# Retention and an ELU feed-forward block on one core: outputs leave PSUM later, M4's input differences come earlier, ELU buffers from two pools, M7's small weights in the second block's first GEMM

## The chip, the core and the metric

The kernel runs on one core of one Trainium2 chip. The metric is device time in microseconds, a median over runs. One execution of the kernel before was profiled; all durations and views below are from that one. In the views PE is TensorE's matmuls, PEld its weight loads, DVE is VectorE, ACT is ScalarE, POOL is GpSimd and SP is SyncE, whose queue (SPq) issues all the DMAs here.

## The reference

```python
# retention: B=4, H=8, S=768, D=64
gamma = 1.0 - 2.0 ** (-5.0 - np.arange(H))
for t in range(S):
    state = gamma * state + k[t] (outer) v[t]
    y[t]  = q[t] @ state / sqrt(D)
# bridge: x = y as (3072 tokens, 512)
h = x @ w_in                       # 512 -> 2048
g = np.where(h > 0.0, h, np.exp(np.minimum(h, 0.0)) - 1.0)
out = g @ w_out                    # 2048 -> 512
```

All of it is in FP32.

## The kernel before

**Blocks.** The 3072 tokens are worked in six blocks of 512 (`tb` 0 to 5). For every block the kernel does the retention of 4 chunks of 128 tokens (scores, states, outputs), then the first GEMM with the ELU, then the second GEMM and the stores. Retention of block `tb + 1` is woven into the GEMMs of block `tb`. The order on every engine is written out by hand: generators (`yield`) are advanced step by step, each engine takes its instructions in program order, and waits follow from the tiles read and written.

**Strassen products.** GEMMs are done with seven products P1 to P7 instead of eight. Block 0 has plain products in its first GEMM and one Strassen level in the second. Block 1 has one level in its first GEMM (four column groups `n` = 0 to 3, functions `first` and `strassen`) and two levels in its second. Blocks 2 to 5 have a first GEMM that is partly two levels deep (`unit`) and a second GEMM of two levels: `second_twice` runs the seven outer products M1 to M7 in the order `ORDER2` = 1, 2, 3, 7, 6, 5, 4 (places `at` = 0 to 6), each an `inner` of seven products with four 128x128x128 FP32 matmuls.

**Inner products and banks.** An `inner` is P1 (bank "a"), P2 ("b"), P6 ("a"), P7 ("d"), P5 ("a"), P3 ("a"), P4 ("d", added to P7). Its P3 and P4, the tail, run after P1 and P2 of the next `inner`. DVE reads bank "d" twice: `res[1,1]` (L1011, shown at L881, the helper `add`) after P5, `res[1,0]` after P4. The loop calls `work(at)` for early and late DVE work: `inputs_of(j)` makes the four input differences `ts` of a coming outer product (L853), `form(j)` differences of whole GEMM results (L790), `next_x` the differences `xt` of the next block's input (L467). `visit(at, where)` puts retention steps in: `outputs` has DVE multiply the PSUM result `y` into `xb` (L397, four operations). `bring` loads the chunks of the block after next (1 MB each) and has POOL scale their v (L285).

**Weights.** The sums of weights that the inner products need ("small weights") are made by DVE, sent to DRAM (`to_send`, `send_small`) and fetched back, 256 KB each, through a ring of 11 tiles `wq` (`fetch_small`, L822 and L827): a fetch is issued when a tile has been used. For the first GEMM of the later blocks `combine_small(j)` makes four sums for j = 2, 3, 7, 4 (L839) and stores 1 MB. M2's and M3's are made in block 1's first GEMM, in tiles `wi` of the pool `stage`; M7's and M4's in block 1's second GEMM, in the memory of `xt`. After the first GEMM the pool is closed and the ring takes its memory:

```python
    early.close()
    ring = ctx.enter_context(tc.tile_pool(name="ring", bufs=RING))
    tpool = ctx.enter_context(tc.tile_pool(name="tpool", bufs=2))
    for _ in range(RING):
        fetch_small()
```

**ELU.** `elu` has ACT make max(-h, 0) and its exponential in a buffer `r`; DVE then joins it with h (L494). `r` comes from `epool`, with three buffers. In `strassen` with `behind` false (n = 1 to 3) the result C11 is P1, copied by ACT to SBUF, plus P2 by DVE (`plus`, L708).

Of the kernel before, what the change touches and what calls it, by code (L numbers as in the profile page):

```python
# [9 lines left out]
FP32 = mybir.dt.float32  # L10
# [8 lines left out]
def kernel(  # L19
# [357 lines left out]
    def outputs(tb, pp):  # L377

        y = [ps_r.tile([P, 2 * 2, 2, D], FP32, name="y", tag="r") for _ in range(2)]
        for x in range(2):  # L380
            for j in range(4):
                pt = raw[tb * CPB + 2 * pp + j // 2][0][:, 1].rearrange("p h c -> p (h c)")
                within(tb, pp, x, j, y, lambda p: pt[:, (x * HP + p) * D :][:, 0:D])
        for other in range(2):
            if not other:
                yield
            else:

                for sub in range(2):
                    seen = epool.tile([P, 8], FP32, name="seen", tag="seen")  # L390
                    nc.vector.tensor_copy(seen.rearrange("p (j x) -> p j x", x=2), y[sub][:, :, :, 0])
                yield
            for x in range(2):
                across(tb, pp, x, other, y)
        i = chunks[tb * CPB + 2 * pp][1]
        for sub in range(2):
            nc.vector.tensor_tensor(  # L397
                out=place_of(x_of(tb)[:, :, 2 * pp * C : 2 * (pp + 1) * C])[:, :, :, sub, :], in0=y[sub],
                in1=place_of(powers[:, :, i * C : (i + 2) * C])[:, :, :, sub, :], op=ALU.mult,
            )  # L400
# [11 lines left out]
    def across(tb, pp, x, other, y):  # L412
        q = raw[tb * CPB + 2 * pp + x][0]
        for u in range(2):
            for a in range(2):
                sub = a ^ other
                n = 4 * pp + 2 * x + sub
                if fresh(tb, n):
                    continue
                for c in range(2):  # L420
                    p = 2 * u + c
                    nc.tensor.matmul(
                        y[sub][rows(c), 2 * a + u, x, :], lhsT=state(tb, n)[rows(a), p, :],
                        rhs=q[rows(a), 0, p, rows(sub)], start=False, stop=True, skip_group_check=True,
                    )
# [56 lines left out]
        while later:  # L482
            later.pop(0)()

    def elu(g, h, depth=1, then=None):


        r = epool.tile([P, 512], FP32, name="r", tag="r", bufs=3)
        e = r if len(h.shape) == 2 else r.rearrange("p (a c) -> p a c", c=P)
        nc.scalar.activation(e, h, AF.Relu, scale=-1.0)  # L490
        nc.scalar.activation(e, e, AF.Exp, scale=-1.0)  # L491

        def last():
            nc.vector.scalar_tensor_tensor(g, e, -1.0, h, ALU.add, ALU.max)  # L494
            if then:
                then()

        while len(later) >= depth:
            later.pop(0)()
        later.append(last)  # L500
# [210 lines left out]
    def strassen(product, use, behind):  # L711


        yield
        pa = bank("a")
        product(1, pa, True)
        m1 = kept(pa)
        yield
        pb = bank("b")
        product(2, pb, True)  # L720
        h = plus(pb, m1)
        if not behind:
            use("C11", h)
        yield
        product(6, pa, False)
        u2 = kept(pa)
        if behind:
            use("C11", h)
        yield
        pd = bank("d")  # L730
        product(7, pd, True)
        yield
        product(5, pa, False)
        u4 = kept(pa)
        use("C22", plus(pd, u4))
        yield "gap"
        product(3, pa, False)
        use("C12", pa)
        yield
        product(4, pd, False)  # L740
        h = plus(pd, u2)
        yield "last"
        use("C21", h)
# [200 lines left out]

    def elu_of(j, r, t):
        g = place(UNITS[j][0][0], r, t)
        elu(g, g, 4)

    def first_one(n, j, ps):

# [232 lines left out]
    def run(steps):  # L1183
        for _ in steps:
            pass
# [12 lines left out]
    for n, _ in enumerate(inner):  # L1198
        if n in (0, 2, 4):
            load(CPB + n // 2)  # L1200
        if n == 4:
            load(CPB + 3)
        if n in (1, 2, 4, 5, 7, 9):
            next_piece(n in (1, 2, 5, 7))
        if n in (3, 5, 7, 9):
            scale_v(CPB + (n - 3) // 2)
        if n == 4:
            run(inputs_of_first(0, [hslot() for _ in range(3)]))
        elif n == 10:
            scores(1, 0)  # L1210
            scores(1, 1)
        elif n == 11:
            states(1, 0)
            states(1, 1)
            next_piece()
            parts = sums_of_pieces(0)
            next(parts)
        elif n == 12:
            outputs_step(1, 0)
            run(parts)  # L1220
            next_piece()
        elif n == 13:
            outputs_step(1, 1)
            smalls = small_of_pieces(0)
            some(smalls, 3)
        elif n == 14:
            outputs_step(1, 2)
            some(smalls, 2)
            decode_all()
        elif n == 15:  # L1230
            run(smalls)
# [43 lines left out]
    def retention_step(tb, step):  # L1275
        if tb >= NTB:
            return
        if step == 0:
            scores(tb, 0)
            scores(tb, 1)  # L1280
        elif step == 1:
            states(tb, 0)
            states(tb, 1)
        elif step < 5:
            outputs_step(tb, step - 2)


    tail = iter(())
    last = held["last"]
    sides = [  # L1290
        itertools.chain(combine_w_in(1), last), itertools.chain(combine_w_in(2), combine_w_in(3)), iter(()), iter(()),
    ]
    smalls = {2: combine_small(2), 3: combine_small(3)}
    some(smalls[2], 1)
    for n in range(NQ):
        if n < 3:
            load(2 * CPB + n)
        if n == 2:
            load(2 * CPB + 3)
        cur = first(n)  # L1300
        for at in range(3):
            next(cur)

        if n in (1, 2):
            some(smalls[n + 1], 1)
        elif n == 3:
            scale_v(2 * CPB, True)
        for _ in tail:
            pass
        for at, s in enumerate(cur):  # L1310
            next(sides[n], None)
            next(sides[n], None)
            if at == 1 and n in (0, 2):
                some(smalls[2 if n == 0 else 3], 2)
            elif at == 1 and n == 3:
                for m in range(1, CPB):
                    scale_v(2 * CPB + m, True)
            if s == "gap":
                break
        for _ in sides[n]:  # L1320
            pass
        tail = cur
        if n in (1, 2):
            run(smalls[n + 1])
        send_small()
# [14 lines left out]
            some(xt_parts[0], 2)  # L1340
        return [begin]

    smalls = {j: combine_small(j, xt_.rearrange("p j a (b c) -> p (j a b) c", c=P).rearrange("p (k f) c -> p k f c", k=4)) for j in (7, 4)}

    def small_part(j):
        def last():
            run(smalls[j])
            send_small()
        return 3 * [lambda: some(smalls[j], 1)] + [last]

    def work_of_second(at):
        i = lambda j: inputs_of(j, ts)
        return [
            ([], i(2)), (i(3), []), (i(7), small_part(7)), (form(6), i(6)), (i(5), small_part(4)), (form(4), i(4)),
            (next_x(), []),
        ][at]

    LOADS = {(4, "end"): (0, 1), (5, "middle"): (2, 3)}
# [1 line left out]
    def visit_of_second(at, where):  # L1360
        if (at, where) == (0, "tail"):
            next(tail)
            next(tail)
        elif (at, where) == (0, "middle"):
            for _ in tail:
                pass
            flush()
        if where == "end" and at < 5:
            retention_step(2, at)
        bring(3, at, where)  # L1370

    def bring(tb, at, where):
# [9 lines left out]
    for tb in range(2, NTB):  # L1382
# [72 lines left out]
        def work_of_second(at):  # L1455
            i = lambda j: inputs_of(j, ts)
            return [
                ([lambda: pop(2)], last_elus + i(2)), ([lambda: pop(2)] + i(3), form(5)), (form(7), i(7)), (form(6), i(6)),
                (i(5), form(4)), ([], i(4)), (next_x() if more else [], []),
            ][at]  # L1460

        def visit_of_second(at, where):
            if (at, where) == (0, "tail"):
                elu_of(3, 0, 0)
                elu_of(3, 1, 1)
                for _ in tail:
                    pass
            elif where == "end" and at in (1, 3, 4) and more:
                retention_step(tb + 1, {1: 2, 3: 3, 4: 4}[at])
            bring(tb + 2, at, where)  # L1470

        tail = second_twice(tb, ts, work_of_second, visit_of_second)
# [51 lines left out]
```

## Time and profile before

| | |
|---|---|
| Median of 3 runs | 644.95 us (644.07 to 645.58) |
| The profiled execution's own time | 639.73 us |
| Its span, first to last instruction | 638.0 us |
| Mean granted clock of TensorE | 1.000 |
| Busy: PE, DVE, ACT | 624.6, 510.0, 264.1 us |
| DMA moved | 146.83 MB, mean 230 GB/s |

A line of the timeline has the start, the duration, the engine, the line of the kernel, the operation, the tile written and the tiles read, shapes, the count of merged instructions, and in brackets the idle time before it with what ended it. A line of waits has the total, the times and the longest. A DMA line has the size and the median time from issue to landing.

### The profile page before, as it was taken

Reading aid. Unit: us, or ns where it says so; the run is one execution under the profiler, and the core shown is the slowest. Engines: PE = TensorE matmul, PEld = TensorE weight load, DVE = VectorE, ACT = ScalarE, POOL = GpSimd, SP = SyncE. Lnnn points to the kernel's source line nnn. Section 1 sums busy time; section 2 is a strip of 40 time slices with the busy share of each in tenths; the row PEclk is TensorE's granted clock in tenths of the full one; section 3 lists DMA queues with packets and bytes.
Section 4 is the critical chain, followed back from the end, with each engine's and each line's share of the span. In section 5 each row is a group of like instructions: output and inputs, shape, how many; then the busy total and the mean of one; then the engine's idle time right before and its main releaser. Section 6 shows DMA issues by size and latency. Waiting matters only on the chain.

```text
span 638.0 us, 16700 instructions
## 1 busy us (share of the span) xinstructions
PE 624.6 (98%) x6870; PEld 564.5 (88%) x6870; DVE 510.0 (80%) x930; ACT 264.1 (41%) x496; POOL 23.6 (4%) x30
## 2 busy tenths in 40 slices
PE   8999999999999989999899999999999999999997
PEld 6864578888899978999898999999899999899997
DVE  5678799989798787499869389988569887469995
ACT  5898645025631112565111367211257311357411
POOL 1021000000000011000002000002000000000000
PEclk9999999999999999999999999999999999999999
DMA  8698669689287997248789136789425888325894
GB/s 320 258 415 295 187 207 269 193 272 327 88 271 234 303 372 275 66 134 257 255 272 395 53 108 194 249 289 398 145 74 169 251 269 263 117 74 166 270 312 138
DMA packets 80794, 146.83 MB, mean 230 GB/s; under 512 B 6864, under 2 KB 32336, under 8 KB 75472
## 3 DMA queue, kind: packets, MB, share of 16 engines
q1 hardware_dynamic: 80720, 145.78, 68.7%
q8 instruction: 54, 0.88, 0.5%
q14 instruction: 20, 0.16, 0.1%
HBM read 122.42 MB, written 23.33 MB: 228 GB/s over the span
## 4 chain that ended last, share of the span: by engine, by line
PE 85%; DVE 9%; issue 2%; ACT 2%; DMA 1%; DVEq 0%
PE pa L984 17%; PE pd L984 9%; PE qa L956 7%; PE pa L896 5%; PE pa L757 4%; PE pb L984 4%; PE pa L956 3%; PE pa L534 3%; PE pb L956 3%; PE x L624 3%; PE pd L896 3%; DVE gC L881 2%; PE pd L757 2%; PE pa L624 2%; PE sc L311 2%; PE y L407 2%
## 5 line engine op out<-in xcount | busy, mean ns | idle before, releaser
L992 ACT COPY ms<-pa 128x128 f32<-128x128 f32 x104 | 27.4, 264 | 146.1 <-PE pa L984 135.5
L984 PE MATMUL pa<-ts,wq 128*128 128x128 f32 x560 | 74.1, 275 | 2.4 <-DMA wq<-scratch_dram 2.4
L984 PE MATMUL pd<-ts,wq 128*128 128x128 f32 x552 | 73.7, 277 | 1.6 <-DVE res L881 1.2
L984 PEld LDWEIGHTS pa<-ts,wq 128*128 128x128 f32 x560 | 68.2, 192 | 2.7 <-issue 2.6
L984 PEld LDWEIGHTS pd<-ts,wq 128*128 128x128 f32 x552 | 67.1, 192 | 3.0 <-DVE res L881 2.9
L984 PE MATMUL pa<-gC,wq 128*128 128x128 f32 x480 | 64.7, 277 | 0.8 <-DVE res L881 0.6
L491 ACT ACTIVATE r<-r 128x512 f32<-128x512 f32 x96 | 60.5, 630 | 3.1
L984 PEld LDWEIGHTS pa<-gC,wq 128*128 128x128 f32 x480 | 58.8, 192 | 2.0 <-DVE res L881 0.8
L490 ACT ACTIVATE r<-gC 128x512 f32<-128x512 f32 x64 | 40.1, 626 | 16.0 <-DVE gC L494 9.4
L881 DVE TENSOR_TENSOR res<-pd,ms 128x128 f32<-128x128 f32 x68 | 19.5, 287 | 32.0 <-ACT ms L992 17.7
L853 DVE TENSOR_TENSOR ts<-gC,ts 128x512 f32<-128x512 f32 x60 | 43.8, 730 | 1.0
L853 DVE TENSOR_TENSOR ts<-gC 128x512 f32<-128x512 f32 x60 | 42.0, 701 | 0.1
L494 DVE SCALAR_TENSOR_TENSOR gC<-r,gC 128x512 f32<-128x512 f32 x64 | 41.1, 682 | 0.6 <-ACT r L491 0.6
L881 DVE TENSOR_TENSOR gC<-pb,gC 128x512 f32<-128x512 f32 x20 | 13.3, 682 | 30.3 <-PE pb L896 30.3
L285 POOL TENSOR_TENSOR chunk<-chunk,vf 128x512 f32<-128x512 f32 x16 | 20.9, 1309 | 410.7 <-DVE ts L853 180.0
L896 PE MATMUL pa<-ts,wq 128*128 128x128 f32 x256 | 34.8, 279 | 0.0
L984 PE MATMUL pb<-gC,wq 128*128 128x128 f32 x240 | 31.9, 276 | 0.0
L896 PEld LDWEIGHTS pa<-ts,wq 128*128 128x128 f32 x256 | 31.1, 191 | 0.5
L984 PEld LDWEIGHTS pb<-gC,wq 128*128 128x128 f32 x240 | 29.4, 192 | 0.0
L1014 ACT COPY res<-pa 128x128 f32<-128x128 f32 x34 | 9.0, 266 | 40.9 <-PE pa L984 40.6
L881 DVE TENSOR_TENSOR res<-res 128x512 f32<-128x512 f32 (+1 forms) x31 | 22.0, 713 | 2.3 <-ACT ms L992 0.5
L790 DVE TENSOR_TENSOR gC<-gC,gC 128x512 f32<-128x512 f32 x36 | 22.4, 683 | 0.0
(274 smaller groups left out, 1259.5 us busy)
## 6 DMA issues: line engine op xcount, KB each, us to landing
wq<-scratch_dram SPq DMA_DIRECT2D x309, 256.0 KB, 4.4
chunk<-in_qkv_dram SPq DMA_DIRECT2D x22, 1024.0 KB, 8.9
wraw<-in_w_dram SPq DMA_DIRECT2D x15, 1024.0 KB, 6.0
out_dram<-res SPq DMA_DIRECT2D x14, 256.0 KB, 4.6
scratch_dram<-gT SPq DMA_DIRECT2D x12, 256.0 KB, 4.4
scratch_dram<-m SPq DMA_DIRECT2D x12, 192.0 KB, 6.3
scratch_dram<-so SPq DMA_DIRECT2D x4, 512.0 KB, 4.7
scratch_dram<-wi SPq DMA_DIRECT2D x2, 1024.0 KB, 6.7
```

The costliest lines, as they stand in the source:

```text
L490: nc.scalar.activation(e, h, AF.Relu, scale=-1.0)
L491: nc.scalar.activation(e, e, AF.Exp, scale=-1.0)
L494: nc.vector.scalar_tensor_tensor(g, e, -1.0, h, ALU.add, ALU.max)
L624: nc.tensor.matmul(X[j][:, d, :], lhsT=w[j][:, d * P : d * P + P], rhs=x[j], start=(n == 0 and d == 0), stop=at_end, skip_group_check=True,)
L757: nc.tensor.matmul(ps[:, fi, :], lhsT=w[:, fi, j2, :], rhs=x[:, j2, :], start=(begin and fi == 0 and j2 == 0), stop=(j2 == 1), skip_group_ ...
L790: nc.vector.tensor_tensor(out=gq[o][:, q], in0=gq[x][:, q], in1=gq[y][:, q], op=ALU.subtract)
L853: sub = lambda o, x, y: nc.vector.tensor_tensor(out=o, in0=x, in1=y, op=ALU.subtract)
L881: nc.vector.tensor_tensor(out=o, in0=x, in1=y, op=ALU.add)
L896: nc.tensor.matmul(ps[:, f, :], lhsT=lhs[f], rhs=xs[j][k], start=(begin and f == 0), stop=True, skip_group_check=True,)
L956: nc.tensor.matmul(ps[:, fi, :], lhsT=w[:, fi, j2, :], rhs=x[:, j2, :], start=(j == 1 and fi == 0 and j2 == 0), stop=(j2 == 1), skip_group ...
L984: nc.tensor.matmul(ps, lhsT=w[:, f, :], rhs=ts[j][k][:, f, :], start=(begin and f == 0), stop=(f == 3), skip_group_check=True,)
L992: nc.scalar.copy(m, ps)
```

## The change

1. `outputs` has one more step, for blocks 1 and later: the four multiplications out of PSUM (L397) are a step of their own. In the second GEMM they come at `(5, "first")`, behind the sum of the M6 result, instead of at the end of `at` = 4.
2. `inputs_of(4)` becomes early work of `at` = 5 instead of late work; in block 1 `form(4)` comes at the end of `at` = 4.
3. `elu_of` takes `r` from `hpool` for the quarters with r != t, and from `epool` for the others.
4. In `strassen` with `behind` false P1 is copied by ACT into bank "b" and P2 is added there by PE; the ELU of C11 reads the bank. P2 comes behind the tail of the group before.
5. `combine_small(7)` is run in block 1's first GEMM, n = 3, in a tile of `stage`, and sent there. In the second GEMM only `combine_small(4)` is left, at the place where M7's was.

```diff
@@ outputs
             for x in range(2):
                 across(tb, pp, x, other, y)
+        if tb:
+            yield
         i = chunks[tb * CPB + 2 * pp][1]
@@ elu
-    def elu(g, h, depth=1, then=None):
-        r = epool.tile([P, 512], FP32, name="r", tag="r", bufs=3)
+    def elu(g, h, depth=1, then=None, pool=None):
+        r = pool.tile([P, 512], FP32, name="r", tag="h") if pool else epool.tile([P, 512], FP32, name="r", tag="r", bufs=3)
@@ strassen
-        m1 = kept(pa)
-        yield
-        pb = bank("b")
-        product(2, pb, True)
-        h = plus(pb, m1)
-        if not behind:
-            use("C11", h)
+        if behind:
+            m1 = kept(pa)
+            pb = bank("b")
+        else:
+            pb = bank("b")
+            nc.scalar.copy(pb, pa)
+        yield
+        product(2, pb, behind)
+        if behind:
+            h = plus(pb, m1)
+        else:
+            use("C11", pb)
@@ elu_of
-        elu(g, g, 4)
+        elu(g, g, 4, pool=None if r == t else hpool)
@@ block 0's loop, n == 14
             outputs_step(1, 2)
+            outputs_step(1, 3)
@@ retention_step
-        elif step < 5:
+        elif step < 6:
             outputs_step(tb, step - 2)
@@ block 1, first GEMM
-        itertools.chain(combine_w_in(1), last), itertools.chain(combine_w_in(2), combine_w_in(3)), iter(()), iter(()),
+        itertools.chain(combine_w_in(1), last), itertools.chain(combine_w_in(2), combine_w_in(3)), iter(()), combine_small(7),
...
-        for at in range(3):
+        for at in range(2 if n else 3):
             next(cur)
...
         for _ in tail:
             pass
+        if n:
+            next(cur)
         for at, s in enumerate(cur):
...
             elif at == 1 and n == 3:
+                run(sides[3])
+                send_small()
                 for m in range(1, CPB):
                     scale_v(2 * CPB + m, True)
@@ block 1, second GEMM
-            ([], i(2)), (i(3), []), (i(7), small_part(7)), (form(6), i(6)), (i(5), small_part(4)), (form(4), i(4)),
-            (next_x(), []),
+            ([], i(2)), (i(3), []), (i(7), small_part()), (form(6), i(6)), (i(5), form(4)), (i(4), []), (next_x(), []),
...
         if where == "end" and at < 5:
             retention_step(2, at)
+        elif (at, where) == (5, "first"):
+            retention_step(2, 5)
@@ blocks 2 to 5, second GEMM
-                (i(5), form(4)), ([], i(4)), (next_x() if more else [], []),
+                (i(5), form(4)), (i(4), []), (next_x() if more else [], []),
...
             elif where == "end" and at in (1, 3, 4) and more:
                 retention_step(tb + 1, {1: 2, 3: 3, 4: 4}[at])
+            elif (at, where) == (5, "first"):
+                retention_step(tb + 1, 5)
```

More of the change, by code (lines that the diff above doesn't have):

```diff
@@ L1290 @@
     sides = [
-        itertools.chain(combine_w_in(1), last), itertools.chain(combine_w_in(2), combine_w_in(3)), iter(()), iter(()),
+        itertools.chain(combine_w_in(1), last), itertools.chain(combine_w_in(2), combine_w_in(3)), iter(()), combine_small(7),
     ]
-    smalls = {2: combine_small(2), 3: combine_small(3)}
+    smalls = {j: combine_small(j) for j in (2, 3)}
     some(smalls[2], 1)
@@ L1341, in next_x, with small_part @@
         return [begin]
-    smalls = {j: combine_small(j, xt_.rearrange("p j a (b c) -> p (j a b) c", c=P).rearrange("p (k f) c -> p k f c", k=4)) for j in (7, 4)}
-    def small_part(j):
+    last_small = combine_small(
+        4, xt_.rearrange("p j a (b c) -> p (j a b) c", c=P).rearrange("p (k f) c -> p k f c", k=4)
+    )
+    def small_part():
         def last():
-            run(smalls[j])
+            run(last_small)
             send_small()
-        return 3 * [lambda: some(smalls[j], 1)] + [last]
+        return 3 * [lambda: next(last_small)] + [last]
     def work_of_second(at):
```

## The prediction

> **What bounds the kernel.** I read the page first, then the waits of PE and of the DMA queue (SP), then the timeline round each place that the diff touches.
>
> ```profile
> PE 624.6 (98%) x6870; PEld 564.5 (88%) x6870; DVE 510.0 (80%) x930; ACT 264.1 (41%) x496; POOL 23.6 (4%) x30
> PE 85%; DVE 9%; issue 2%; ACT 2%; DMA 1%; DVEq 0%
> ```
>
> The busy line and the chain by engine: TensorE sets the time, and the number of its matmuls does not change. So only its waits can be won or added.
>
> ```profile
> PE pa L984 <- DMA wq<-scratch_dram: 2.4, 1, 2.4
> PE pd L984 <- DVE res L881: 1.2, 3, 0.5
> SPq L827 <- DMA scratch_dram<-wi: 4.9, 1, 4.9
> ```
>
> Waits (total, times, longest). PE waits once for a weight tile (2.4 us, at 231 in block 1) and a little for bank "d" to be read. The third line is the warning: the first ring fetch stood behind the landing of a stored `wi` tile.
>
> **1. M7's weights in the first GEMM (n = 3): +7.5 us.** In the built order of the changed kernel SP issues M7's store right ahead of the ring's first fetch, and that fetch waits on the store's landing, because the ring lies in the memory of the closed pool `stage`. M3's store has that place now:
>
> ```profile
> 167.95 0.68 DVE L839 TENSOR_TENSOR wi<-w_s,wi 128x512 f32<-128x512 f32 x1
> 168.66 0.33 SPq L656 DMA_DIRECT2D scratch_dram<-wi  x1
> 174.04 0.80 SPq L827 DMA_DIRECT2D wq<-scratch_dram  x2
> 178.01 1.05 PE L984 MATMUL pa<-gC,wq 128*128 128x128 f32 x8
> ```
>
> ```profile
> scratch_dram<-wi SPq DMA_DIRECT2D x1, 1024.0 KB, 5.3
> wq<-scratch_dram SPq DMA_DIRECT2D x2, 256.0 KB, 2.7
> scratch_dram<-xt SPq DMA_DIRECT2D x1, 1024.0 KB, 4.8
> ```
>
> The timeline, and issue to landing of these DMAs: store 168.7, landed 174.0, fetch, landed 176.6, first use at 177.8 (the weight load ahead of the 178.01 row). Slack 1.2 us.
>
> When does M7's store leave? Its four sums stand on DVE behind the ELU of n = 2's C21. PE runs P1(3), then n = 2's last two products, which end at 171.3 (each 1.73; today P2(3) is between and they end at 173.0). DVE then does the C21 sum at 171.3, C12's ELU 171.9, the two L769 sums 172.6 and 173.35, C21's ELU 174.0, and M7's four at 0.61 a start from 174.6: done 177.2. Store 5.3, fetch 2.7, start of PE 0.1: 185.3 instead of 177.8. PE has nothing else: the product stands ahead in its order. +7.5; low end 6.9 (the 4.8 row), high end 9.3 (a fetch at the page's median of 4.4). The ring's later tiles come 0.7 apart and are wanted 0.9 apart, so nothing more is lost.
>
> The wait's length raises the clock question. After the idle start of the program four 128-column matmuls take 1.11 us, where eight take 1.06 later; that slow pace runs from 1.45 to about 5.8 us and loses half of 4.4, 2.2 us. After the 2.4 us wait at 231 eight take 1.13, full pace.
>
> ```profile
> 5.14 1.11 PE L339 MATMUL pa<-so,chunk 128*128 128x128 f32 x4
> ```
>
> A wait of 7.5 us lies between these rows, so 0 to 2.2; I take the middle, +1.1. The Trainium skill ("TensorE: Matmul & The Clock Gate", Part 1: The HAM clock gate) says more: an idle window of about 3.4 us halves the clock, and about 3.4 us of work restores it. By that the loss would be an estimated 1.7 to 3.4 us, and the whole sum 0.6 to 2.3 higher.
>
> **2. M4's small sums where M7's were (block 1).** The 1 MB store ahead of the chunk loads at 222.7 goes, and with it the fetch wait at 231. The store moves on SP to 207.3, ahead of the fetches that M7's precedes today without a wait of PE, and the 2.5 us of sums move on DVE from 220 to 204.6; `form(4)` (2.5 us) comes up to their old place. What is won here is reckoned in 3, because a new wait comes first.
>
> **3. Outputs out of PSUM later, M4's input differences earlier (second GEMM, at = 4 to 6).** Block 2 today:
>
> ```profile
> 325.77 1.16 PE L984 MATMUL pa<-gT,wq 128*128 128x128 f32 x8
> 327.71 2.47 DVE L397 TENSOR_TENSOR xb<-y,etab 128x512 f32<-128x512 f32 x4
> 330.30 0.28 DVE L881 TENSOR_TENSOR res<-pd,ms 128x128 f32<-128x128 f32 x1
> 330.63 0.97 PEld L984 LDWEIGHTS pd<-ts,wq 128*128 128x128 f32 x8 [0.32 <-DVE res L881]
> 333.02 0.29 DVE L881 TENSOR_TENSOR res<-pd,ms 128x128 f32<-128x128 f32 x1 [1.65 <-ACT ms L992]
> 333.23 1.10 DVE L853 TENSOR_TENSOR ts<-gC 128x512 f32<-128x512 f32 x1
> 335.19 1.37 POOL L285 TENSOR_TENSOR chunk<-chunk,vf 128x512 f32<-128x512 f32 x1 [1.40 <-DVE ts L853]
> 335.58 1.53 DVE L853 TENSOR_TENSOR ts<-gC,ts 128x512 f32<-128x512 f32 x1
> 337.56 0.97 PEld L984 LDWEIGHTS pd<-ts,wq 128*128 128x128 f32 x8 [0.60 <-DVE res L881]
> ```
>
> At at = 5 the order is P1 (325.77), P2, at 4's P3 and P4, P6, P7, P5, then at 6's P1, P2, and at 5's P3, P4. P7 (its weight load is the row at 330.63) waits for the read of bank "d" at 330.30, which stands behind the four L397 (0.3 us); a second P7 waits at 337.56 because the `ts` sums were stretched beside POOL. Both waits go, as meant. But the changed DVE order at at = 5 is: sums of at 4, four L397, four `ts`, and only then `res[1,1]`, the second read of bank "d" after P5. At 5's P4 adds into that bank and waits for it.
>
> Without POOL, from P1's start: P4 of at 4 ends at +3.85, its read +3.9, `res<-res` +4.3, L397 +4.9 to +7.3, `ts` +7.3 to +9.9, the read +9.8 to +10.05, P4 +10.1, second P7 two products and one refill later, +12.0. Block 4 has no chunk loads; its second P7 starts at +11.2 (539.04 against 527.83): +0.8.
>
> With POOL (blocks 1 to 3) the `ts` sums are pinned: the first ends after POOL's first product, the last after its second, as today at 337.11. The read follows at 337.05 to 337.3, P4 at 337.4 instead of 335.2, second P7 at +13.5 against +11.8: +1.7. Block 3: `ts` end 438.25, P4 +11.8, second P7 +13.7 against 438.70 − 426.68 = 12.0: +1.7. Block 1: P7 at 234.65 − 220.57 = +14.1 today (0.4 for the bank, 2.6 for the fetch); I take +13.6: −0.5. Sum −0.5 + 1.7 + 1.7 + 0.8 = +3.7. Low end: `ts` never stretched, +12.0 everywhere: −2.1 + 0.2 + 0 + 0.8 = −1.1. High end: one more stretched operation (0.4) in three blocks, +4.9.
>
> **4. ELU buffers from two pools (blocks 2 to 5): −1.6 us.**
>
> ```profile
> 282.03 0.63 ACT L490 ACTIVATE r<-gC 128x512 f32<-128x512 f32 x1 [1.39 <-DVE gC L494]
> 283.23 0.58 ACT L910 COPY pb<-pa 128x512 f32<-128x512 f32 x1
> 283.87 1.16 PE L896 MATMUL pb<-xb,w_s 128*128 128x128 f32 x8
> ```
>
> ACT waits 1.39 us for the third ELU buffer; behind it stands the copy into "pb", and PE starts 0.33 late for it (0.23 wait, 0.10 refill), then 0.2 for the next ACT copy. At most 0.53 a block, four blocks: −2.1. DVE is the next late one at 281 to 283, so I take 0.4 each: −1.6; end 0.
>
> **5. P2 after the tail, C11 summed in PSUM: 0.** ACT copies "pa" to "pb" instead of to SBUF; the copy (0.58) is hidden by two products of 3.45 us, and three DVE sums of 0.61 go. The extra step of block 1's `outputs` in the first block runs right behind the step before it, so its order stays. C11 of n = 3 is ready only at 180.1 instead of 172.4, and the second inner product reads it: 1.3 us if the ring wait of part 1 did not cover it.
>
> **Sum.** 7.5 + 1.1 + 3.7 − 1.6 = +10.7 us on the profiled execution's 639.73 (span 638.0): 650.4. The median of the runs shown, 644.95, is 5.2 above that execution; the added waits are the same there: 655.6.
>
> **Rivals.**
> *No new wait for bank "d"*: if bank reads came in time, the second P7 would start at +10.8 (twelve products of 0.89 and a refill); blocks 1 to 4 would save 3.3, 1.0, 1.2 and 0.4, and the sum would be 7.5 + 1.1 − 5.9 − 1.6 = +1.1: 646.1. For it: no P4 waits today. Against it: the built order puts eight operations of 0.61 us, 4.9 us, between P4's old and new reads.
> *The store does not hold the ring* (faster): M7's store would have landed by 177.8. For it: DVE idles for 1.9 and 1.0 us at 166 to 170. Against it: the sums stand behind C21's ELU, in order. With zero wait C11 still costs 1.3; with the terms of 3 and 4 at their low ends the sum is 1.3 − 1.1 − 2.1 = −1.9: 643.0. With a ring wait w above 1.3 the sum is w − 3.2, so this decides for faster by over 0.2% once w is below 1.9 us.
> *The clock halves for the whole 4.4 us*: +1.1 more, 656.7, inside the range.
> *The edits do not do what they say*: the new ELU buffers share `hpool` with `m7` and the results; if a buffer were held by an output DMA, part 4 would be 0 or above: 657.2 or more. The output stores of block 2 are issued by 349 and the next unit's tiles come 15 us later, so it is unlikely.
>
> **How the numbers follow.** My forecast 0.80 (with either clock), no bank wait 0.10, no ring hold 0.05, the ELU rival 0.05. The forecast's ends are 644.95 + 6.9 + 0 − 1.1 − 2.1 = 648.7 and 644.95 + 9.3 + 2.2 + 4.9 = 661.4; 650.0 to 661.0 leaves out the two low rivals and little else. A difference under 0.2% (1.3 us) can't be told from none here. Slower 0.91: forecast, ELU rival and part of the first rival; same 0.04; faster 0.05.
>
> **What would show it.** Right: the first L984 product near 185 with a wait of 7 us for `wq`, after a `wi` store at 177; no fetch wait in block 1's end; P4 of at 5 waiting 1 to 2.5 us for `res` in blocks 1 to 4 and P7 not waiting; the ACT wait of 1.39 gone. Wrong: a first fetch before 178, or P4 starting on time.

## The result

The changed kernel takes 653.4 us (median of 4 runs, 652.47 to 656.6) beside 645.2 for the kernel before: a ratio of 1.0139 (95% interval 1.010 to 1.0178), 8 to 9 us slower. A second comparison gave 1.0134 (1.009 to 1.0178). The forecast was 655.6 in a range of 650.0 to 661.0. The profiled execution took 652.47 us with a span of 650.7. Line numbers have moved: the adds of L881 are now L888, the products of L984 L991, the differences of L853 L860, the outputs of L397 L399, the small sums of L839 L846, the fetches L829 and L834. A ratio is taken over all runs and is not the quotient of the two medians.

The page of the changed kernel, its busy line and its chain by engine:

```profile
PE 626.1 (96%) x6870; PEld 567.2 (87%) x6870; DVE 506.6 (78%) x927; ACT 263.9 (41%) x496; POOL 22.2 (3%) x30
PE 91%; DVE 4%; DMA 2%; issue 2%; DVEq 0%; SPq 0%
```

The count of TensorE's instructions is the same and its busy time is 1.5 us longer, while the span grew by 12.7. So most of the time, 11.2 us, was added in waits. DVE has three sums less, as the change says, and is 3.4 us less busy; TensorE's waits did not fall with it. The waits of the changed kernel (total, times, longest):

```profile
PEld pd L991 <- DVE res L888: 7.4, 5, 2.4
PE pd L991 <- DVE res L888: 6.5, 4, 2.2
PE pa L991 <- DMA wq<-scratch_dram: 6.1, 1, 6.1
```

Before, PE had 2.4 us for `wq` and 1.2 for bank "d". Now it waits 6.1 us for the first tile of the ring and four times for bank "d", up to 2.2 us. These are the two waits that were forecast.

**The ring.** The timeline of the changed kernel round the first product of block 1's second GEMM:

```profile
177.49 0.68 DVE L846 TENSOR_TENSOR wi<-w_s,wi 128x512 f32<-128x512 f32 x1
178.20 0.33 SPq L658 DMA_DIRECT2D scratch_dram<-wi  x1
182.26 0.80 SPq L834 DMA_DIRECT2D wq<-scratch_dram  x2
185.27 0.98 PE L991 MATMUL pa<-gC,wq 128*128 128x128 f32 x3 [6.10 <-DMA wq<-scratch_dram]
```

M7's last sum ends at 178.2, the store leaves with it and lands at 182.07, the fetch leaves at 182.26 and lands at 184.93, and the product starts 0.3 us later. The chain sums, store, fetch, product is as the prediction drew it; only the store is shorter (3.9 us for 5.3).

**The clock.** Windows behind the two longest waits (PE, PEld, DVE, ACT and POOL busy with counts, granted clock, DMA share, GB/s):

```profile
185.20:187.00 1.80, 1.73 (x8) 1.76 (x9) 0.00 (x0) 0.00 (x0) 0.00 (x0) 0.50 0.81 156
187.00:189.00 2.00, 2.00 (x12) 1.98 (x12) 0.00 (x0) 0.27 (x1) 0.00 (x0) 0.57 0.91 289
189.00:191.00 2.00, 2.00 (x11) 1.77 (x10) 0.89 (x2) 0.30 (x1) 0.00 (x0) 1.00 1.03 397
345.00:347.00 2.00, 2.00 (x12) 2.00 (x13) 0.65 (x3) 0.00 (x0) 0.00 (x0) 0.68 1.10 449
347.00:349.00 2.00, 2.00 (x11) 2.00 (x11) 1.07 (x2) 0.27 (x1) 0.00 (x0) 0.50 0.98 406
```

The granted clock is 0.5 for 3.4 us behind the wait of 6.1 us, as feared, and again behind the wait of only 2.2 us in block 2, which the prediction had not priced.

**Bank "d".** The same place in block 2 (P1 of `at` = 5 starts at 333.60):

```profile
338.48 2.48 DVE L399 TENSOR_TENSOR xb<-y,etab 128x512 f32<-128x512 f32 x4
340.38 1.04 POOL L285 TENSOR_TENSOR chunk<-chunk,vf 128x512 f32<-128x512 f32 x1 [89.86 <-DMA chunk<-in_qkv_dram]
340.87 1.09 DVE L860 TENSOR_TENSOR ts<-gC 128x512 f32<-128x512 f32 x1
342.83 1.36 POOL L285 TENSOR_TENSOR chunk<-chunk,vf 128x512 f32<-128x512 f32 x1 [1.41 <-PE pa L991]
343.21 1.53 DVE L860 TENSOR_TENSOR ts<-gC,ts 128x512 f32<-128x512 f32 x1
344.66 0.28 DVE L888 TENSOR_TENSOR res<-pd,ms 128x128 f32<-128x128 f32 x1
345.00 1.45 PE L991 MATMUL pd<-ts,wq 128*128 128x128 f32 x8 [2.20 <-DVE res L888]
```

`res[1,1]`, the read of bank "d" at 344.66, was ready to run at 340.4 (ACT's copy of P5 had ended). It stands behind four outputs and four differences, two of them stretched while POOL works, and P4 at 345.00 waits for it.

### The profile page after: what moved, and what is told of

Its sections match the earlier page's. It is cut to its first block, busy times and chain, and to the rows that moved or that the text cites. A ratio compares the mean times of both kernels' runs of the same rounds, so it can differ in the third digit from the quotient of the medians.

```text
span 650.7 us, 16691 instructions
## 1 busy us (share of the span) xinstructions
PE 626.1 (96%) x6870; PEld 567.2 (87%) x6870; DVE 506.6 (78%) x927; ACT 263.9 (41%) x496; POOL 22.2 (3%) x30
## 4 chain that ended last, share of the span: by engine, by line
PE 91%; DVE 4%; DMA 2%; issue 2%; DVEq 0%; SPq 0%
PE pa L991 18%; PE pd L991 9%; PE pa L903 9%; PE qa L963 6%; PE pd L903 4%; PE pb L991 4%; PE pa L764 4%; PE pa L963 3%; PE pa L536 3%; PE pb L963 3%; PE x L626 3%; PE pb L903 2%; PE pa L626 2%; PE kv L351 2%; PE y L409 2%; PE sc L311 2%
## 5 line engine op out<-in xcount | busy, mean ns | idle before, releaser
L991 PE MATMUL pd<-ts,wq 128*128 128x128 f32 x552 | 74.4, 278 | 6.5 <-DVE res L888 6.5
L991 PE MATMUL pa<-ts,wq 128*128 128x128 f32 x560 | 74.8, 277 | 0.0
L991 PEld LDWEIGHTS pd<-ts,wq 128*128 128x128 f32 x552 | 68.0, 194 | 7.5 <-DVE res L888 7.4
L991 PE MATMUL pa<-gC,wq 128*128 128x128 f32 x480 | 65.8, 280 | 7.2 <-DMA wq<-scratch_dram 6.1
L991 PEld LDWEIGHTS pa<-ts,wq 128*128 128x128 f32 x560 | 69.1, 194 | 0.1
L991 PEld LDWEIGHTS pa<-gC,wq 128*128 128x128 f32 x480 | 59.5, 194 | 8.8 <-issue 7.1
L888 DVE TENSOR_TENSOR res<-pd,ms 128x128 f32<-128x128 f32 x68 | 19.5, 287 | 37.7 <-PE pd L991 25.5
L860 DVE TENSOR_TENSOR ts<-gC,ts 128x512 f32<-128x512 f32 x60 | 43.5, 726 | 1.0
L860 DVE TENSOR_TENSOR ts<-gC 128x512 f32<-128x512 f32 x60 | 41.4, 690 | 1.2 <-DMA scratch_dram<-wi 1.0
L888 DVE TENSOR_TENSOR gC<-pb,gC 128x512 f32<-128x512 f32 x20 | 13.3, 681 | 30.3 <-PE pb L903 30.3
L285 POOL TENSOR_TENSOR chunk<-chunk,vf 128x512 f32<-128x512 f32 x16 | 19.5, 1219 | 424.9 <-PE pa L991 277.6
L991 PE MATMUL pb<-gC,wq 128*128 128x128 f32 x240 | 32.5, 280 | 0.0
L991 PEld LDWEIGHTS pb<-gC,wq 128*128 128x128 f32 x240 | 30.1, 197 | 0.0
L888 DVE TENSOR_TENSOR res<-res 128x512 f32<-128x512 f32 (+1 forms) x31 | 21.9, 710 | 1.9
```

The source lines that it names most:

```text
L860: sub = lambda o, x, y: nc.vector.tensor_tensor(out=o, in0=x, in1=y, op=ALU.subtract)
L888: nc.vector.tensor_tensor(out=o, in0=x, in1=y, op=ALU.add)
L991: nc.tensor.matmul(ps, lhsT=w[:, f, :], rhs=ts[j][k][:, f, :], start=(begin and f == 0), stop=(f == 3), skip_group_check=True,)
```

## The experiments

Ratios are to runs of the kernel before on the same chip, which has medians of 645.4 to 646.6 us in these comparisons.

### The changed kernel again

> The changed kernel again, on the chip of the next runs and with more runs. Theory (its cost is fixed by the two waits): PE waits 6 us for wq after the first GEMM of block 1 and 1.8, 2.3, 1.8 and 1.1 us for bank d at P4 of at = 5 in blocks 1 to 4, as in the first trace; +8 us or a little over on the kernel before, ratio 1.011 to 1.015. Rival (the first four runs were slow by chance): the waits differ by over 1 us from the first trace, ratio 1.008 or below.

Measured 653.5 us, ratio 1.0134 (1.009 to 1.0178). PE's start-to-start excess at `wq` is 6.5 us, at P4 2.7, 2.7, 1.8 and 1.1 us in blocks 1 to 4. The cost is fixed; which of the shorter waits is followed by the slow clock is not (here again the one of block 2).

### M7's sums in n = 2

```diff
-    sides = [..., iter(()), combine_small(7)]
+    sides = [..., iter(()), iter(())]         # and smalls has 7 too
     elif at == 1 and n == 3:
-        run(sides[3])
-        send_small()
...
         run(smalls[n + 1])
+    if n == 2:
+        run(smalls[7])
     send_small()
```

> The changed kernel (653.4 us), with the four M7 sums put behind M3's, in column group n = 2, instead of in n = 3; nothing else differs. Theory (M7's store, which lands late, holds the ring's first fetch): the sums end near 172 instead of 178.2, the store lands near 176, PE's wait for wq (6.1 us) falls under 1 us, and the granted clock is 1.00 in the first inner product instead of 0.5; about 6.2 + 1.9 us less, 645.3 (644 to 647). Rival 1 (something else in the closed pool or in the queue holds the fetch): the wait stays over 4 us, 650 to 653. Rival 2 (the sums now delay DVE's reads of PSUM in n = 2): the wait for wq goes, but PE waits 1 to 2 us for a bank between 172 and 178, 646 to 648.

Measured 645.7 us, ratio 1.0008 (0.9975 to 1.0041): 8 us less than the changed kernel, as the theory said. The wait did not fall under 1 us, though, but to 2.2. The timeline of this version:

```profile
171.51 0.33 SPq L658 DMA_DIRECT2D scratch_dram<-wi  x1
177.47 0.80 SPq L834 DMA_DIRECT2D wq<-scratch_dram  x2
180.43 0.79 PE L991 MATMUL pa<-gC,wq 128*128 128x128 f32 x5 [1.93 <-DVE gC L496]
```

The store left 6.7 us sooner, but 2.5 us behind M3's, and took 5.8 us; the fetch still leaves when it lands, and lands itself at 180.08. The product starts 0.3 us after that, as in the changed kernel. The row names C11's ELU, which ended at the same time; the run with P2 alone (below), where it starts 2.1 us before that ELU ends, shows that the first product does not need it. No wait for a bank came up at 172 to 178 (rival 2), and the clock stayed at 1.00.

### Filling the wait

```diff
     for _ in range(RING):
         fetch_small()
+    for _ in range(6):
+        nc.tensor.matmul(idle, lhsT=some_w[:, 0:P], rhs=some_w[:, 0:512], start=True, stop=True, ...)
```

> The changed kernel (653.4 us), with six matmuls of 512 columns whose result nobody reads ahead of the first inner product of block 1's second GEMM; they take 6 x 0.86 = 5.1 us of the 6.4 us in which PE waits there. Theory (the slow pace after the wait is TensorE's clock, halved by the idle time): the wait ends at the same moment, the granted clock after it is 1.00 instead of 0.5, and the 1.9 us lost in the first 4 us after it are gone: 651.5. Rival (the slow pace comes from tiles or weights that arrive late, not from the clock): pace and time stay, 653.4; if the six matmuls delayed the products, 654 or more.

The timeline and the window behind the wait:

```profile
178.39 5.31 PE L1347 MATMUL idle<-w_a 128*128 128x512 f32 x12
184.44 1.13 PE L991 MATMUL pa<-gC,wq 128*128 128x128 f32 x8 [0.73 <-DMA wq<-scratch_dram]
```

```profile
184.40:186.40 2.00, 1.96 (x17) 2.00 (x18) 0.00 (x0) 0.27 (x1) 0.00 (x0) 1.00 0.58 124
```

Measured 647.9 us, ratio 1.0051 (1.002 to 1.0081). The product still starts 0.3 us behind its tile, and eight matmuls take 1.13 us at once, with the clock at 1.00. So the slow pace was the clock and the idle time made it. The time fell by 5.5 us, more than the 1.9 expected; the intervals leave room for 3, and the mean granted clock of these 12 runs (median 0.997, against 0.991 over the ten runs of the changed kernel) accounts for some 3.5, the 1.9 among them, by the slope given in the last section. The rest is open. The profiled execution, at 653.33 us, was the slowest of the 12: three of its later waits for bank "d", of 2.7 us each, were followed by the half clock.

### Four experiments on bank "d"

**M4's differences late again.**

```diff
-    (i(5), form(4)), (i(4), []), (next_x(), []),
+    (i(5), form(4)), ([], i(4)), (next_x(), []),
```

> The changed kernel (653.4 us), with M4's four input differences put back behind the read res[1,1] of bank d (late work of at = 5), as before; the outputs stay at their new place. Theory (P4 of at = 5 waits because that read stands behind outputs and differences): the P4 waits of 1.7, 2.3, 1.7 and 1.0 us in blocks 1 to 4 go, and with the one of block 2 a loss of 1.0 us to the clock; P7 of at = 6 waits 0.5 to 0.9 us for bank d in blocks 1 to 3 as it did before: 7.7 - 2.2 = 5.5 less, 648 (647 to 649.5). Rival (the outputs alone, late, make P4 wait): P4 waits of 1 us or more stay in all four blocks, 650 to 652.

```profile
341.23 0.28 DVE L888 TENSOR_TENSOR res<-pd,ms 128x128 f32<-128x128 f32 x1
342.88 0.97 PEld L991 LDWEIGHTS pd<-ts,wq 128*128 128x128 f32 x8
343.81 1.53 DVE L860 TENSOR_TENSOR ts<-gC,ts 128x512 f32<-128x512 f32 x1
345.46 0.27 DVE L888 TENSOR_TENSOR res<-pd,ms 128x128 f32<-128x128 f32 x1
345.79 0.97 PEld L991 LDWEIGHTS pd<-ts,wq 128*128 128x128 f32 x8 [0.77 <-DVE res L888]
```

Measured 648.8 us, ratio 1.0038 (1.0014 to 1.0063), as the theory had it. In block 2 the read now runs at 341.23 and P4 (342.88) does not wait; the differences fall on POOL instead and P7 waits 0.77 us at 345.79 (0.60 in the kernel before).

**The outputs back, the differences early.**

```diff
         if where == "end" and at < 5:
             retention_step(2, at)
-        elif (at, where) == (5, "first"):
-            retention_step(2, 5)
+            if at == 4:
+                retention_step(2, 5)
```

(and the same for the later blocks)

> The changed kernel (653.4 us, ratio 1.0134), with the four multiplications out of PSUM put back at the end of at = 4, as before; M4's input differences stay early. Theory (each of the two moves alone leaves DVE in time for P4; only both together put eight operations ahead of the read): the differences start 2.5 us sooner, mostly before POOL's products; P4 of at = 5 waits under 0.3 us in all four blocks, P7 of at = 5 waits 0.3 us again: 6.7 + 0.8 (clock) - 1.0 = 6.5 less, ratio 1.0035. Rival (the early differences alone make P4 wait, since POOL pins their end): P4 waits of 1.4 us or more stay in blocks 1 to 3, ratio 1.009 to 1.011.

Measured 646.7 us, ratio 0.9997 (0.9967 to 1.0027). P4 of `at` = 5 does not wait in any block; P7 of `at` = 5 waits 0.3 us in each, as expected. So neither move alone makes the wait, only the two together. The gain is 8.8 us by the ratios, 6.8 by the medians, for the 6.5 expected; the expected ratio lies just outside the interval, and the trace shows no third term.

**Three differences and one.**

```diff
-    (i(5), form(4)), (i(4), []), (next_x(), []),
+    (i(5), form(4)), ([], x4[:3]), (x4[3:] + next_x(), []),     # x4 = i(4), kept
```

> The changed kernel (653.4 us), with three of M4's four input differences behind the read res[1,1] of bank d (late work of at = 5) and the fourth behind the reads of at = 6's start (early work of at = 6); only P4 of at = 6 needs the fourth. Theory (the waits for bank d are the order of DVE around its two reads): neither P4 of at = 5 nor P7 of at = 6 waits for DVE in blocks 1 to 4: 6.7 us of waits and 1.0 us of clock go, 645.7 (644.5 to 647). Rival (POOL stretches whatever DVE does there, and the stretch lands on the reads): waits of 0.5 to 0.9 us per block stay, 647.5 to 649.

Measured 648.5 us, ratio 1.0022 (0.9998 to 1.0046). P4 of `at` = 5 and P7 of `at` = 6 no longer wait for bank "d" in any of the four blocks; 0.2 and 0.4 us are left in blocks 1 and 2 at P6 of `at` = 6, which writes bank "a". The theory's 645.7 us would be a ratio of 1.001, the rival's times 1.003 and above; the time lies between, and the trace decides for the theory. What is missing stands in two other places: 2.0 us of waiting for a fetch at 441, and 0.5 us more at the end, where the last block wants the fourth difference sooner. The second is mended in the version below by splitting only where a block follows.

**P7's old waits and the ELU, from the kernel before.** The kernel before, with the outputs later, the differences three and one, and the two ELU pools:

> The kernel before, with the outputs a step later, M4's input differences three and one (as in the version with three edits) and the ELU buffers from two pools; M7's and M4's small weights and P2 stay as before. Theory (the gains add up by place): the waits for bank d at P7 (0.42, 0.31 + 0.58, 0.31 + 0.72, 0.29 us in the trace of before) and four times 0.45 us at the ELU go, the fetch wait of 2.6 to 3.6 us in block 1 stays: 2.6 + 1.8 = 4.4 less, ratio 0.993. Rival (what follows takes them back: weight fetches come next in line, the block 1 wait grows by the 0.4 us won ahead of it): ratio 0.996 or above.

```profile
DVE res L883 <- PE pd L986: 21.1, 25, 1.4
PE pa L986 <- DMA wq<-scratch_dram: 3.1, 3, 1.5
```

Measured 641.3 us, ratio 0.9937 (0.9909 to 0.9964), the 0.993 expected. DVE waits for the products now (first line); among PE's waits of 1 us or more none is left for bank "d", and 3.1 us for `wq` in three parts, the longest of 1.5. The number is the expected one, but not every term is: the fetch wait of block 1 is 1.3 us and not 2.6 to 3.6, and PE waits 1.5 us at 229 for `form(4)`, which the theory did not have.

### The ELU buffers alone

```diff
-        r = epool.tile([P, 512], FP32, name="r", tag="r", bufs=3)
+        r = pool.tile([P, 512], FP32, name="r", tag="h") if pool else epool.tile([P, 512], FP32, name="r", tag="r", bufs=3)
...
-        elu(g, g, 4)
+        elu(g, g, 4, pool=None if r == t else hpool)
```

> The kernel before, and of the change only the ELU buffers from two pools. Theory: the ACT wait of 1.4 us in each unit goes, and with it the 0.23 us of PE behind the copy into pb and the next 0.2: 0.4 to 0.5 us in each of blocks 2 to 5, 1.6 to 2.0 less, ratio 0.997. Rival (DVE is next in line): ACT's wait goes, PE's stays, ratio 1.000. Rival 2 (the new buffers share a pool with results and m7, which now wait): 1.001 or above, with a wait of ACT or DVE for such a buffer.

```profile
285.19 0.58 ACT L910 COPY pb<-pa 128x512 f32<-128x512 f32 x1
286.11 1.16 PE L896 MATMUL pa<-xt,wq 128*128 128x128 f32 x8
287.10 1.06 PE L896 MATMUL pb<-xb,w_s 128*128 128x128 f32 x8
```

Measured 645.0 us, ratio 0.9971 (0.994 to 1.0001). In the timeline the copy into "pb" stands 0.9 us ahead of the product before it, where it stood 0.6 behind, and the product that reads it starts without a wait. 0.4 to 0.5 us a block, four blocks.

### M7's weights alone, and P2 alone

M7 alone is the kernel before with M7's four sums and its store in n = 3 and M4's sums at `at` = 2.

> The kernel before, and of the change only M7's small weights in n = 3 and M4's where M7's were. Theory: PE waits about 6 us for wq after the first GEMM and loses 1.5 to 2 us to the clock; the fetch wait of 2.6 us near 239 goes, and 0.4 us for bank d ahead of it: +5 us, ratio 1.008. Rival (the fetch wait there is the chunk loads' doing, not the 1 MB store's): it stays at 2 us or more, +8 us, ratio 1.012.

```profile
PE pa L984 <- DMA wq<-scratch_dram: 7.2, 1, 7.2
PEld pd L984 <- DVE res L881: 1.8, 5, 0.7
```

Measured 651.5 us, ratio 1.0089 (1.006 to 1.0119). The one wait for `wq` left is the new one, 7.2 us; the fetch wait at the end of block 1, which every trace with M7's weights in the old place has (2.6 us in that of before, 3.6 in those of the ELU and of P2 alone, 1.3 in the fourth run on bank "d"), is gone. The chunk loads stayed where they were, so it was the 1 MB store there, moved with its sums, that made it.

P2 alone is the kernel before with P2 behind the tail and C11 summed in PSUM.

> The kernel before, and of the change only the first GEMM's P2 behind the tail and C11 summed in PSUM. Theory (C11 of n = 3 is finished by DVE behind the sum of C22, near 180): the first L984 product waits for gC instead of starting at 177.8, about 2 us, and half the time the clock drops after it (0.7 on average): ratio 1.003 to 1.004. Rival (the copy is hidden and three DVE sums less pay for it): no wait there, ratio 1.000 or 0.999.

```profile
177.85 1.05 PE L989 MATMUL pa<-gC,wq 128*128 128x128 f32 x8
178.67 0.69 DVE L708 TENSOR_TENSOR h<-pd,m 128x512 f32<-128x512 f32 x1 [2.38 <-ACT m L703]
179.28 0.68 DVE L494 SCALAR_TENSOR_TENSOR gC<-r,pb 128x512 f32<-128x512 f32 x1
180.03 0.97 PEld L989 LDWEIGHTS pb<-gC,wq 128*128 128x128 f32 x8 [1.31 <-issue]
```

Measured 648.5 us, ratio 1.0025 (0.9994 to 1.0055). The first product, which the theory had waiting, starts on time at 177.85. The second one reads C11 of n = 3, whose ELU ends at 179.96 because DVE takes it behind C22's sum, and waits 1.3 us. (The row says "issue": the profile found no semaphore for it; its start 0.1 us behind the ELU's end says more.) The time alone, at the edge of what can be told, would not settle it.

### The changed kernel with three edits

The edits: M3's sums at the start and M7's in the middle of n = 2; a `flush()` in n = 3 ahead of the scalings, so that DVE finishes C11's ELU first; and the differences three and one, in the last block all four late.

```diff
+    elif n == 2:
+        run(smalls[3])
+        send_small()
...
-        some(smalls[2 if n == 0 else 3], 2)
+        some(smalls[2 if n == 0 else 7], 2 if n == 0 else 4)
     elif at == 1 and n == 3:
-        run(sides[3])
-        send_small()
+        flush()
...
-    (i(5), form(4)), (i(4), []), (next_x() if more else [], []),
+    (i(5), form(4)), ([], x4[:3] if more else x4), (x4[3:] + next_x() if more else [], []),
```

> The changed kernel with three edits: M3's sums stand at the start and M7's in the middle of column group n = 2, one place earlier each; DVE finishes the ELU of C11 of n = 3 ahead of three scalings, not behind C22's sum; M4's input differences stand three behind res[1,1] and one at the start of at = 6 (in the last block all four behind res[1,1]). Theory: no wait for wq or C11 at the first inner product, no waits for bank d in blocks 1 to 4; against before, its fetch wait at 231 (2.6 us), seven waits for bank d (2.9 us together) and four ELU waits of 0.45 go: 645.5 - 7.3 = 638 (636.5 to 640), ratio 0.989. Rival 1 (the weight fetches are next in line, as for 2.0 us at 441 in the run with the differences split): fetch waits of 2 us or more somewhere in blocks 1 to 3, 640 to 643. Rival 2 (the earlier sums delay DVE's reads of PSUM in n = 2): PE waits for a bank between 160 and 178, 640 to 642.

```profile
168.43 0.33 SPq L658 DMA_DIRECT2D scratch_dram<-wi  x1
172.47 1.47 SPq L834 DMA_DIRECT2D wq<-scratch_dram  x2
180.15 1.05 PE L991 MATMUL pa<-gC,wq 128*128 128x128 f32 x8
333.95 0.28 DVE L888 TENSOR_TENSOR res<-pd,ms 128x128 f32<-128x128 f32 x1
335.61 0.97 PEld L991 LDWEIGHTS pd<-ts,wq 128*128 128x128 f32 x8
337.39 0.97 PEld L991 LDWEIGHTS pd<-ts,wq 128*128 128x128 f32 x8
```

Measured 639.0 us, ratio 0.9891 (0.9847 to 0.9935), for 638 expected. The first tile lands at 175.40, nearly 5 us before its product; in block 2 neither P4 (335.61) nor P7 (337.39) waits, and in blocks 1 and 3 only P6 of `at` = 6 does, 0.4 and 0.5 us. The earlier sums do cost something: PE waits 0.7 us at 166 for a bank.

> The version with three edits again, on the same chip, beside the kernel that lacks its move of M7's weights. Theory (the move, once its store lands in time, is worth the fetch wait of block 1 and what the clock loses after it): 0.988 to 0.990, 2.6 us or more under the other. Rival (the move is worth nothing): both the same within 1 us.

Measured 638.6 us, ratio 0.9902 (0.9867 to 0.9938), beside 641.3 for the kernel without the move of M7's weights, which also lacks the change of P2 and its `flush()`. The difference of 2.7 us is expected in sign and size, but the trace of that kernel has a fetch wait of only 1.3 us in block 1 and the 1.5 us for `form(4)`. The two intervals overlap, so what the move alone is worth is not shown. Rival 1 of the first run holds in part: in this second trace PE waits 2.1 us for a fetch from 438 to 440, with the slow clock behind it; in the first trace there is no such wait.

## Why the prediction was right

**Part 1, the ring: +7.5, measured +6.3.** The place and the time of M7's sums were right: end at 177.2, measured 178.2 in a trace in which PE itself was 1.0 us late from a stall at 24.6, taken up below. So was the fetch. The store was mis-sized: 5.3 us came from one row, M3's. (The low end, 6.9, is 7.0 by its own row, 0.5 less.) In the traces here 1 MB of `wi` took 4.2 to 5.3 us in M3's place and 3.8 to 3.9 in M7's.

**The clock: +1.1, measured +1.7 here, and as much again where no term stood.** Behind the wait of 6 to 7.5 us the first trace lost 1.7 us, the other five with that wait unfilled 1.9 to 2.5; the middle of 0 to 2.2 was too low. Its upper end came from slow rows at the program's start, beside which the profile's granted clock reads 1.00: they show a pace and not its cause. What failed is that only the longest wait was asked this question. The 2.2 us wait of block 2 cost 1.7 more, though a 2.4 us wait at 231 in the trace of before had cost nothing; the last section says why. The Trainium skill ("TensorE: Matmul & The Clock Gate", Part 1: The HAM clock gate) speaks of a free-running window and of about 3.4 us of idle time. The first fits what is seen here: the clock was halved for 3.41 us or a multiple of it. The second does not: waits of 2.04 us already halved the clock. The estimate from that page in the prediction, 1.7 to 3.4 us, holds all six losses behind the long wait.

**Part 3, bank "d": +3.7, measured +1.5 without the clock.** By block, change of the second P7 after P1 of `at` = 5: forecast -0.5, +1.7, +1.7, +0.8, measured -1.3 (14.08 to 12.75), +2.6 (11.79 to 14.35, some 1.2 of it the slow clock: +1.3), +0.7 (12.02 to 12.75) and +0.8 (11.21 to 12.03). In block 2 P4 was expected at +11.6 and came at +11.4, in block 4 at +10.1 and +10.1. In block 3 it came at +10.9 for +11.8: POOL did not hold the differences as long as in block 2. With that, blocks 1, 2 and 3 were priced too high by 0.8, 0.4 and 1.0: 2.2 together. The fetch wait of block 1 went, as part 2 of the prediction has it.

**Part 4, the ELU: -1.6, measured -0.4 to -0.5 in each of four blocks**, together -1.9.

**Part 5: 0, and 1.3 us behind a ring that does not wait.** It was 1.3 in the run with P2 alone.

**The sum.** 10.7 - 1.2 (store) + 2.3 (clock) - 2.2 (bank "d") - 0.3 (ELU) = 9.3, and the two ratios give 8.6 to 9.0 us. The errors of the clock and of bank "d" cancel; that the sum came out so close is in part luck. The spans of the two traces differ by more, 12.7. The other 3.4 cannot be put down to the change: 2.8 are stalls within rows of small 64x64 products (`y`) at 24.6 and 415 us, for which the profile names no releaser and which kernels without most of these edits show as well (that of before at 315, the run with the ELU alone at 319 and 409); the rest are smaller differences at 206 and 323.

**The rivals.** *No new wait for bank "d"* and *the store does not hold the ring* are both refuted by the first trace, and by what happened when the order on DVE and the time of the store were changed. *The edits do not do what they say* is refuted by the ELU run. The clock's rival was nearer to the truth than the middle.

## What to carry to other kernels

When a step is moved on an in-order engine, list what now stands between an operation and the one that waits for it: here two moves together put eight operations (4.9 us, and 6.2 beside POOL in block 2) ahead of a 0.3 us read that releases a bank, and neither alone made P4 wait. A transfer moved to just ahead of a pool's reuse holds the next owner of that memory; started some 10 us sooner, as in the version with three edits, it left no wait there. And a wait of some 2 us or more on TensorE should be priced with the clock behind it: 1.7 us for each halved window of 3.4 us, and between 2 and 3 us as a chance, because where the windows lie differs from one execution to the next.

## What was not expected of the hardware

**Waits and the clock.** Over the fourteen traces, waits of PE behind 100 us can be set beside the matmul time lost in the next 7 us:

| wait (excess over the normal start-to-start) | waits | followed by over 1 us lost |
|---|---|---|
| 1.5 to 2.0 us | 12 | 0 |
| 2.03 to 2.74 us | 29 | 15 |
| 3.57 to 7.5 us | 8 | 8 |

Each loss was 1.6 to 2.6 us. In between, the same wait in the same place goes either way from one execution to the next. What decides is how it lies to a grid of time. Between 100 us and the last products the clock is halved 23 times, in twelve of the traces, each time for 3.41 us, twice or once three times that; and the changes within a trace lie whole numbers of 3.413 us apart, to about 1 ns. Two waits, cut along that grid, which in the trace of before is set by its one change, at the end (columns as in the windows above):

```profile
342.30:345.71 3.41, 1.21 (x11) 1.02 (x10) 2.84 (x5) 0.27 (x1) 1.36 (x1) 1.00 1.08 415
345.71:349.12 3.41, 3.41 (x18) 3.41 (x18) 1.58 (x3) 0.27 (x1) 0.00 (x0) 0.50 1.02 419
228.82:232.23 3.41, 2.43 (x22) 2.24 (x20) 3.38 (x6) 0.27 (x1) 1.49 (x1) 1.00 1.00 413
232.23:235.65 3.42, 1.96 (x17) 1.99 (x18) 2.45 (x5) 0.27 (x1) 1.44 (x1) 1.00 1.01 358
235.65:239.06 3.41, 3.41 (x26) 3.20 (x24) 2.09 (x4) 0.85 (x2) 0.00 (x0) 1.00 1.02 396
```

The first two rows are the changed kernel: the 2.2 us wait lies in one window, and the next is at half clock, though PE was busy again. The other three are the kernel before: a boundary cuts the 2.4 us wait into 1.0 and 1.5 us of idle time, and the clock stays. Over the fourteen traces, behind 100 us and at full clock, all 20 windows with 1.89 us or more without a matmul were followed by a halved one, 3 of the 6 with 1.78 to 1.86, and none with less. Behind the long ring wait the halved stretch begins within the wait, so only half of what is left of it is lost: in the first trace it runs from 181.87 to 188.69, of which 3.4 us lie behind the product's start at 185.27, and 1.7 us were lost.

**Run to run.** This goes with about half of the variance between runs of this kernel. Over 97 runs of the kernel before, those with a mean granted clock of 0.997 or more (29) have a median of 643.9 us, those with 0.993 or less (25) 646.8; the slope is 0.6 us for each 0.001 of clock, which is what one halved window gives by itself (1.7 us for a mean clock lower by 0.0026). The profiled execution of before, with a clock of 1.000 and 639.73 us, is faster than every one of the 97; its clock explains part of the 5.2 us between it and the median, on which the prediction set its sum. The other part fits the stalls in rows of `y` products, of which that trace has one of 2.0 us, and most others two of 1.5 to 2.6; what makes them is not shown.

**One store, several durations.** The same 1 MB store, alone in the queues, took 3.8 us in one place and up to 5.3 in another. One row is not a price.
